# Expert and converted output weights with four consecutive rows per partition

## Chip, cores and metric

The kernel runs on one core of a Trainium2 chip. The metric is device microseconds of one execution, as the median of the runs.

## What is computed

The reference, cut to what matters (the feed-forward weights are float64 in the inputs, the rest float32):

```python
# cross read: B=8, H=8, S=512 tokens, Ns=32 state rows, D=64
a  = softmax(x @ state.T / 8);  xread = a @ state
a2 = softmax(state @ x.T / 8);  sread = a2 @ x
x  = concat([xread, sread])                  # 4352 tokens x 512
# gated unit: d_ff = 1536
xn = x / rms(x) * rms_g
x  = silu(xn @ w_gate) * (xn @ w_val) @ w_out
# soft mixture: 8 experts x 4 slots, hidden 1024
logits = x @ phi                             # 32 slots
d = softmax over tokens;  slot_input = d.T @ x
for e in range(8):
    slot_out[e] = relu(slot_input[e] @ w1[e]) @ w2[e]
out = softmax over slots(logits) @ slot_out
```

## The kernel before

The 4352 tokens are worked through in nine groups: eight of 512 tokens, one for each batch (in steps of 128 tokens by 512 hidden columns), and one of 256 tokens with the state rows that were read. For each step TensorE forms gate and value products, ScalarE and VectorE make the gated hidden rows, TensorE transposes them, and the logits against the slots are accumulated. `w_out` is never applied to the tokens: the slots' sums are taken over hidden rows (`acc`, 128 x 3 x 512), and `w_out` is applied once, to the 32 slots. This is where the change begins.

After the last group comes the tail (L996 and after), which runs in this order:

- `acc` is turned by products with `dsel` (L1024: three chunks of four products, whose stationary side is a block of 128 columns of `acc`), giving `shT`. The converted `w_out` (`take(("wo", c))`, L1030) is applied to it. The result `sip` holds the 32 slots by 512 columns in four partial rows.
- `sip` is turned by four products with `r32` (L1058, stationary side a block of 128 columns of `sip`). L1062 puts each expert's slots into `sinE[e]`, with zeros elsewhere.
- The experts run in four pairs. `expert_in(p)` (L1081) multiplies two experts' slots by `w1`: 16 products of 32 slot columns by 512 hidden columns, on TensorE's four groups of 32 columns. `expert_turn(p)` (L1096) transposes the copies `HP` (eight transposes of 128 columns, stationary side a block of `HP`), `expert_out(p)` (L1112) multiplies by `w2` into `so_ps`. The order is: `expert_in(0)`, then for each p `expert_in(p + 1)`, `expert_turn(p)`, `expert_out(p - 1)`, and at the end `expert_out(3)`.
- The slots' outputs are spread to all tokens (`out0`, `out_group`) and written out.

The weights for the tail come in 35 loads of 1 MB each: three of the converted `w_out` from its place in device memory, 16 of `w1`, 16 of `w2`. They are all issued on SP's queue by `prefetch` (L700) in the order of the list `loads` (L686 to L695). A load is issued when the buffer that it takes has been released: `take` marks the buffer, `refill` issues the next load. Each load puts 512 rows by 512 columns on 128 partitions as four rows of 512 for each partition. Which rows these are is what changes:

```python
# L711, L713, L715: row 128 k + p goes to partition p, place k
src = w_out32[k[1] * 512 : (k[1] + 1) * 512, :].rearrange("(k p) d -> p k d", p=P)
src = w1[k[1], :, k[2] * 512 : (k[2] + 1) * 512].rearrange("(k p) f -> p k f", p=P)
src = w2[k[1], k[2] * 512 : (k[2] + 1) * 512, :].rearrange("(k p) d -> p k d", p=P)
```

Since float32 products are issued as two passes, one `mm` of float32 operands shows as two matmuls and two weight loads in the profile. A transpose shows as one of each.

Of the kernel before, what the change touches and what calls it, by code (L numbers as in the profile page):

```python
# [20 lines left out]
def kernel(  # L21
# [62 lines left out]
    def mm(o, lhsT, rhs, start=True, stop=True):  # L84
        nc.tensor.matmul(out=o, lhsT=lhsT, rhs=rhs, start=start, stop=stop)  # L85

# [1 line left out]
    ident = small("ident", [P, P])  # L88
    make_identity(nc, ident)
    r32 = small("r32", [P, 32])  # L90
# [5 lines left out]
    rs_magic = small("rs_magic", [P, NT], dt=I32)  # L96
    nc.vector.memset(rs_magic.bitcast(F32), RS_MAGIC)

    # Bits of float64's high word, read as float32: the least and greatest that float32 holds.
    EXP_LO, EXP_HI = 2.0 ** -15, 122879.984375  # L100

    def keep_warm(n):
        """Products that nobody reads, so that a short wait doesn't slow the array's clock."""
        ps = mmps()
        for _ in range(n):
            tc.keep_in_program_order(nc.tensor.matmul(out=ps[:, :P], lhsT=ident, rhs=ident, start=True, stop=True))

    def transpose(o, i):
        nc.tensor.transpose(o, i, ident)  # L109

# [1 line left out]
    XN, T = {}, {}  # L112

    def load_xt(b):
# [15 lines left out]
    phis = asmall("phis", [P, 4, NSLOT])  # L130
    nc.scalar.dma_start(out=phis, in_=phi)

# [1 line left out]
    dram = ctx.enter_context(tc.tile_pool(name="dram", bufs=1, space=bass.MemoryType.DRAM))  # L134
    w_out32 = dram.tile([DFF, DM], F32, name="w_out32")
    bits = {
# [84 lines left out]
                )  # L221


# [1 line left out]
    def att_g(b):  # L225
        stTg = small("stTg", [P, P], bufs=3)
        ins = nc.gpsimd.tensor_tensor(
# [173 lines left out]
    RINV = {}  # L401

    def rinv_from(g, ss, n):
        """(ss / DM + 1e-6) ** -0.5, by Newton's steps from the halved exponent."""
        y = small("rinv", [P, NT], bufs=3)[:, :n]
        v = small("rv", [P, NT])[:, :n]
        a = small("ra", [P, NT])[:, :n]
        i = small("ri", [P, NT], dt=I32)[:, :n]
        nc.vector.tensor_scalar(
            out=v, in0=ss, scalar1=1.0 / DM, scalar2=1e-6, op0=ALU.mult, op1=ALU.add  # L410
        )
        nc.vector.tensor_scalar(  # L412
            out=i, in0=v.bitcast(I32), scalar1=1, scalar2=-1,
            op0=ALU.logical_shift_right, op1=ALU.bitwise_xor,
        )
        nc.gpsimd.tensor_tensor(out=y.bitcast(I32), in0=i, in1=rs_magic[:, :n], op=ALU.add)  # L416
        for _ in range(3):
            nc.vector.tensor_tensor(out=a, in0=y, in1=y, op=ALU.mult)
            nc.vector.scalar_tensor_tensor(
                out=a, in0=a, scalar=-0.5, in1=v, op0=ALU.mult, op1=ALU.mult  # L420
            )
            nc.vector.scalar_tensor_tensor(
                out=y, in0=a, scalar=1.5, in1=y, op0=ALU.add, op1=ALU.mult
            )
        RINV[g] = y

# [1 line left out]
    WP = {}  # L428

    def sw(b, c, gv):  # L430
# [14 lines left out]
            )  # L445
        WP[b, c, gv] = t

# [1 line left out]
    HH, HT, LGP = {}, {}, {}  # L449
    xsg_t = {}  # L450
    wphi = small("wphi", [P, NF, 32])
# [56 lines left out]
                stop=(c == NC - 1),  # L508
            )

# [1 line left out]
    sacc = small("sacc", [P, 1])  # L512
    mrun = small("mrun", [P, 1])
    Q = {}
# [103 lines left out]
            out=v, in0=v, in1=cs[:, :n].unsqueeze(2).to_broadcast([P, n, 32]), op=ALU.mult  # L618
        )

# [1 line left out]
    wphi_done, WPP = set(), {}  # L622

    def wphi_part(c, j):
        """phi' @ w_out' for half of the d_model rows of a 512-wide chunk; j = 1 ends the chunk."""
        wt = WOT.pop((c, j))
        ps = misc()
        for k in range(2):
            mm(ps[32 * k : 32 * k + 32, :], phis[:, 2 * j + k, :], wt[:, k, :])
        if j == 0:  # L630
            WPP[c] = k2("wpp")
            nc.vector.tensor_copy(WPP[c][:64], ps[:64])
            return
        wp = WPP.pop(c)
        nc.vector.tensor_tensor(out=wp[:64], in0=ps[:64], in1=wp[:64], op=ALU.add)
        ps = misc()
        for q in range(4):
            mm(ps[:, 32 * q : 32 * q + 32], wp[:64, q * P : (q + 1) * P], r32[:64])
        nc.vector.tensor_copy(
            wphi[:, 4 * c : 4 * c + 4, :], ps[:, :P].rearrange("p (q s) -> p q s", q=4)  # L640
        )
        wphi_done.add(c)

# [1 line left out]
    def sread_prep():  # L645
        xg = k8("xg").rearrange("p a f -> p (a f)")[:, : 4 * B * NS].rearrange(
            "p (k n) -> p k n", k=4
# [23 lines left out]
    WH = {}  # L671

    def w_split(gv, c):
        """The weights' chunk in two float32r parts."""
        w = W.pop((gv, c))
        h, l = k8("wh", F32R), k8("wl", F32R)
        for k in range(4):
            nc.scalar.copy(h[:, k, :], w[:, k, :])
            nc.vector.tensor_tensor(
                out=l[:, k, :], in0=w[:, k, :], in1=h[:, k, :].bitcast(F32), op=ALU.subtract  # L680
            )
        WH[gv, c] = h, l

# [1 line left out]
    EW = {}  # L685
    loads = []  # L686
    for c in range(NC):
# [1 line left out]
    NPAIR = NE // 2  # L689
    for p in range(NPAIR + 2):  # L690
        if p < NPAIR:
            loads += [("w1", 2 * p + i, j) for j in range(2) for i in range(2)]
        if p >= 2:
            loads += [("w2", 2 * (p - 2) + i, j) for i in range(2) for j in range(2)]
    loads.reverse()  # L695
# [2 lines left out]
    ew_home, ew_free = {}, []  # L698

    def prefetch(n, home=None):  # L700
        """Start the next n loads, in slots of `big` (home None) or of the experts' pool."""
        for _ in range(n):
            if not loads:
                return
            k = loads.pop()
            if home is None:
                t = k8("ew")
            else:
                t = home.tile([P, 4, 512], F32, tag="ew", bufs=4, name="ew_" + "_".join(map(str, k)))
            if k[0] == "wo":  # L710
                src = w_out32[k[1] * 512 : (k[1] + 1) * 512, :].rearrange("(k p) d -> p k d", p=P)  # L711
            elif k[0] == "w1":
                src = w1[k[1], :, k[2] * 512 : (k[2] + 1) * 512].rearrange("(k p) f -> p k f", p=P)  # L713
            else:
                src = w2[k[1], k[2] * 512 : (k[2] + 1) * 512, :].rearrange("(k p) d -> p k d", p=P)  # L715
            nc.sync.dma_start(out=t, in_=src)
            EW[k], ew_home[k] = t, home

# [5 lines left out]
        while ew_free:  # L724
            prefetch(1, ew_free.pop(0))

# [1 line left out]
    def conv1(n=1):  # L728
        wconv(n)
        if len(to_load) > 6 and (to_load[-1][0] < 2 or len(RAW) < 3):  # L730
# [39 lines left out]
        rinv_from(0, T[0, "ss"], NT)  # L770

    pinned.append(1)
# [1 line left out]
    def rinv(b):  # L774
        rinv_from(b, T[b, "ss"], NT)

# [22 lines left out]
    for s, units in enumerate(stages):  # L799
# [65 lines left out]
            at(16, 1, att_a4, 2)  # L865
        else:
            g = s
            o = 4 if s == 1 else 0  # the first unit's place in the usual twelve
            if s == 1:
                at(0, 1, conv1)  # L870
                at(0, 2, wphi_part, 2, 1)
# [121 lines left out]
        prefetch(PU[u])  # L993
    assert not plan

# [1 line left out]
    h_T(*pend[0])  # L997
    lg_mm(*pend[0])
    post1(gs)
# [21 lines left out]
    for c in range(NC):  # L1021
        ps = mmps()
        for q in range(4):
            mm(ps[:, 32 * q : 32 * q + 32], acc[:, c, q * P : (q + 1) * P], dsel)  # L1024
        (nc.vector.tensor_copy if c % 2 else nc.scalar.copy)(
            shT[:, 4 * c : 4 * c + 4, :], ps[:, :P].rearrange("p (q s) -> p q s", s=32)
        )
# [27 lines left out]
    c_exp(gs)  # L1055
    ps = misc()
    for k in range(4):
        mm(ps[:, 32 * k : 32 * k + 32], sip[:, k * P : (k + 1) * P], r32)  # L1058
    # each expert's inputs of its own slots, zero in the others'
    for e in range(NE):  # L1060
        es = slice(4 * e, 4 * e + 4)
        nc.vector.tensor_tensor(  # L1062
# [16 lines left out]
    HP = {}  # L1079

    def expert_in(p):  # L1081
        """The first products of two experts: slots of one have zeros in the other."""
        for j in range(2):
            ps = mmps()
            for i in range(2):
                e = 2 * p + i
                wt = take(("w1", e, j))
                for k in range(4):
                    mm(
                        ps[32 * k : 32 * k + 32, :], sinE[e][:, k, :], wt[:, k, :],  # L1090
                        start=(i == 0), stop=(i == 1),
                    )
            HP[p, j] = hp1[:, 2 * (p % 2) + j, :]
            (nc.scalar.copy if j else nc.vector.tensor_copy)(HP[p, j], ps)

    def expert_turn(p):  # L1096
        hr = small("hr", [P, 8, 8], bufs=2)
        for j in range(2):
            ps = misc()
            for q in range(4):  # L1100
                transpose(ps[:, q * P : (q + 1) * P], HP[p, j][:, q * P : (q + 1) * P])
            HP.pop((p, j))
            v = ps.rearrange("p (f k s) -> p f s k", f=4, k=4)[:, :, 8 * p : 8 * p + 8, :]
            nc.vector.reduce_sum(hr[:, 4 * j : 4 * j + 4], v, axis=AX.X)
        for i in range(2):
            e = 2 * p + i
            nc.vector.tensor_scalar(
                out=hzs[e][:, :, 4 * e : 4 * e + 4], in0=hr[:, :, 4 * i : 4 * i + 4],
                scalar1=0.0, scalar2=None, op0=ALU.max,
            )  # L1110
# [10 lines left out]
                    )  # L1121

    def out_prep():
        """Group 0's weights of the slots, in two parts, each four times."""
        ch = k8("ch", F32R)[:, 0, :P].rearrange("p (t s) -> p t s", s=32)
        cs = k8("cs")[:, :2, :].rearrange("p i (t q s) -> p i t q s", t=NT, q=4)
        cr = k8("csT", F32R)
# [83 lines left out]
    c_turn(1)  # L1211
    expert_out(NPAIR - 1)

    # so_ps still has the four parts of each slot's sum; group 0 takes it as it is
    s4 = k8("s4", F32R)
    s4_h, s4_l = s4[:, 0, :], s4[:, 1, :]
    nc.scalar.copy(s4_h, so_ps)
# [86 lines left out]
```

## Time and profile before

| what | us |
|---|---|
| median of 3 runs (lowest, highest) | 690.29 (690.04, 691.79) |
| profiled execution: span from first to last instruction | 691.4 |
| TensorE busy in that span | 640.3 (93%) |
| VectorE busy | 407.7 (59%) |
| ScalarE busy | 388.9 (56%) |
| weight loads of TensorE busy (beside its products) | 410.6 (59%) |
| DMA: 92.55 MB, share of 16 engines on the main queue | 36.3% |

The profiled execution's own time is its span: nothing that is shown lies around it, and the span lies inside the range of the three runs. In the profile, PE is TensorE's products, PEld its weight loads, DVE VectorE, ACT ScalarE, POOL GpSimd and SP the queue that issues the transfers. L1024 is line 1024 of the kernel before. `mm<-dsel,acc` names the output, the moving and the stationary operand, in this order. The chain of waits is followed back from the last instruction to what released it; the time of a stretch on it is time that sets the end.

### The profile page before, as it was taken

Reading aid. Unit: us, or ns where it says so; the run is one execution under the profiler, and the core shown is the slowest. Engines: PE = TensorE matmul, PEld = TensorE weight load, DVE = VectorE, ACT = ScalarE, POOL = GpSimd, SP = SyncE. Lnnn points to the kernel's source line nnn. Section 1 sums busy time; section 2 is a strip of 40 time slices with the busy share of each in tenths; the row PEclk is TensorE's granted clock in tenths of the full one; section 3 lists DMA queues with packets and bytes.
Section 4 is the critical chain, followed back from the end, with each engine's and each line's share of the span. In section 5 each row is a group of like instructions: output and inputs, shape, how many; then the busy total and the mean of one; then the engine's idle time right before and its main releaser. Section 6 shows DMA issues by size and latency. Waiting matters only on the chain.

```text
span 691.4 us, 11529 instructions
## 1 busy us (share of the span) xinstructions
PE 640.3 (93%) x4560; PEld 410.6 (59%) x4560; DVE 407.7 (59%) x852; ACT 388.9 (56%) x632; POOL 129.1 (19%) x158
## 2 busy tenths in 40 slices
PE   6789988999989999999999999999999999999980
PEld 4346646456555766566676658665666676753350
DVE  6979996762687457554835673575455355342160
ACT  5477943754776459546764765496446366311170
POOL 2634554230032101110201021011000000002430
PEclk9799998999999999999999999999999999999995
DMA  9940246031042011203110320020081307999957
GB/s 349 404 193 2 101 152 236 1 129 63 1 156 96 5 47 77 96 5 122 45 53 1 122 92 1 19 105 31 1 309 58 122 1 257 326 334 382 344 186 331
DMA packets 33581, 92.55 MB, mean 134 GB/s; under 512 B 1912, under 2 KB 4088, under 8 KB 30712
## 3 DMA queue, kind: packets, MB, share of 16 engines
q1 hardware_dynamic: 33240, 91.76, 36.3%
q8 instruction: 36, 0.59, 0.4%
q14 instruction: 17, 0.14, 0.1%
q10 hardware_dynamic: 288, 0.07, 0.0%
HBM read 79.76 MB, written 12.06 MB: 133 GB/s over the span
## 4 chain that ended last, share of the span: by engine, by line
PE 75%; DVE 7%; ACT 5%; issue 1%; POOL 0%; DVEq 0%; ACTq 0%
PE mm L85 42%; PE misc L85 17%; PE misc L109 10%; PE lg L85 3%; PE so L85 2%; DVE wp L443 1%; DVE h L479 1%; ACT wp L442 1%; ACT L471 1%; DVE wo L200 1%; ACT sg L471 1%; DVE wo L208 1%; DVE rm L272 1%; ACT sT L285 0%; DVE wo L204 0%
## 5 line engine op out<-in xcount | busy, mean ns | idle before, releaser
L85 PE MATMUL mm<-wp,A 128*128 128x512 f32 x1152 | 304.9, 405 | 0.4 <-DVE h L479 0.4
L85 PEld LDWEIGHTS mm<-wp,A 128*128 128x128 f32 x1152 | 207.3, 189 | 64.1 <-issue 24.5
L479 DVE SCALAR_TENSOR_TENSOR h<-mm,rinv,sg 128x512 f32<-128x512 f32 x102 | 76.1, 747 | 131.1 <-PE mm L85 93.6
L471 ACT ACTIVATE sg<-mm,rinv 128x512 f32<-128x512 f32 x102 | 70.2, 690 | 81.0 <-PE mm L85 78.0
L85 PE MATMUL misc<-w,stTg 64*32 64x512 f32 x768 | 81.7, 618 | 17.6 <-DVE wp L443 7.5
L442 ACT CAST wp<-misc 128x512 fp32r<-128x512 f32 x96 | 51.7, 591 | 65.2 <-PE misc L85 63.1
L443 DVE TENSOR_TENSOR wp<-misc,wp 128x512 fp32r<-128x512 f32 x96 | 61.8, 682 | 26.6 <-ACT wp L442 26.1
L109 PE MATMUL misc<-ident,h 128*128 128x128 f32 x408 | 61.3, 277 | 1.9 <-DVE h L479 0.7
L490 ACT COPY hT<-misc 128x512 f32<-128x512 f32 x86 | 49.2, 580 | 24.6 <-PE misc L109 20.5
L109 PEld LDWEIGHTS misc<-ident,h 128*128 128x128 f32 x408 | 50.1, 142 | 18.2 <-DVE wp L443 3.3
L85 PEld LDWEIGHTS misc<-w,stTg 64*32 64x32 f32 x768 | 15.5, 106 | 67.7 <-issue 22.1
L308 POOL TENSOR_TENSOR a<-a,asum 128x1024 f32<-128x1024 f32 x7 | 13.4, 1917 | 132.4 <-issue 84.8
L471 ACT ACT_TABLE_LOAD x28 | 35.9, 1283 | 3.7 <-PE mm L85 3.2
L416 POOL TENSOR_TENSOR rinv<-ri,rs_magic 128x4 int32<-128x4 int32 (+1 forms) x9 | 1.8, 198 | 173.2 <-DVE ri L412 173.2
L397 ACT ACTIVATE misc<-misc 128x512 f32<-128x512 f32 x32 | 18.7, 585 | 26.9 <-PE misc L85 18.8
L212 POOL TENSOR_TENSOR w<-w,raw 128x512 int32<-128x512 int32 x20 | 28.1, 1418 | 27.6 <-ACT wp L442 7.2
L85 PE MATMUL mm<-wh,xsg 128*128 128x512 f32 x96 | 31.7, 399 | 0.0
L85 PE MATMUL misc<-bd,A 128*128 128x256 f32 x192 | 29.6, 292 | 1.5 <-DVE A L380 1.5
L212 POOL TENSOR_TENSOR wo<-wo,raw 128x512 int32<-128x512 int32 x18 | 24.8, 1387 | 32.7 <-DVE wo L208 23.3
L85 PE MATMUL lg<-hT,wphi 128*32 128x512 f32 (+1 forms) x216 | 27.4, 577 | 1.5 <-ACT hT L490 1.5
L85 PEld LDWEIGHTS misc<-bd,A 128*128 128x128 f32 x192 | 25.5, 191 | 5.1 <-DVE A L380 2.2
L85 PE MATMUL misc<-h,ET 128*32 128x512 f32 x204 | 26.4, 596 | 0.0
(196 smaller groups left out, 831.8 us busy)
## 6 DMA issues: line engine op xcount, KB each, us to landing
ew<-in_w_dram SPq DMA_DIRECT2D x27, 1024.0 KB, 8.1
xT<-in_x_t_dram SPq DMA_DIRECT2D x8, 1024.0 KB, 5.5
xn<-in_x_n_dram SPq DMA_DIRECT2D x8, 1024.0 KB, 7.7
raw<-in_w_val_dram SPq DMA_DIRECT2D x6, 1024.0 KB, 16.6
raw<-in_w_out_dram SPq DMA_DIRECT2D x6, 1024.0 KB, 5.0
out_dram<-ob SPq DMA_DIRECT2D x6, 1024.0 KB, 12.1
ew_w<-in_w_dram SPq DMA_DIRECT2D x5, 1024.0 KB, 10.4
raw<-in_w_gate_dram SPq DMA_DIRECT2D x4, 1024.0 KB, 14.2
```

The lines of the kernel that those rows point to most:

```text
L85: nc.tensor.matmul(out=o, lhsT=lhsT, rhs=rhs, start=start, stop=stop)
L109: nc.tensor.transpose(o, i, ident)
L200: nc.vector.tensor_scalar(out=dst[:, h], in0=dst[:, h], scalar1=EXP_LO, scalar2=EXP_HI, op0=ALU.max, op1=ALU.min,)
L208: nc.vector.scalar_tensor_tensor(out=a[:, h], in0=hi[:, h], scalar=-0x40000000, in1=a[:, h], op0=ALU.bitwise_and, op1=ALU.bitwise_or,)
L212: nc.gpsimd.tensor_tensor(out=a[:, h], in0=a[:, h], in1=rnd[:, h], op=ALU.add)
L308: (eng or nc.gpsimd).tensor_tensor(out=a3, in0=a3, in1=asum.unsqueeze(2).to_broadcast([P, 32, 32]), op=ALU.mult)
L397: nc.scalar.activation(out=ps, in_=ps, func=AF.Square, accum_out=T[b, "ss"][:, t : t + 1])
L442: nc.scalar.copy(t[:, r, 0, :], ps)
L443: nc.vector.tensor_tensor(out=t[:, r, 1, :], in0=ps, in1=t[:, r, 0, :].bitcast(F32), op=ALU.subtract)
L471: nc.scalar.activation(out=sg, in_=ps, func=AF.Silu, scale=RINV[g][:, t : t + 1])
L479: nc.vector.scalar_tensor_tensor(out=HH[g, c][:, t, :], in0=ps, scalar=RINV[g][:, t : t + 1], in1=sg, op0=ALU.mult, op1=ALU.mult,)
L490: (nc.vector.tensor_copy if on_dve else nc.scalar.copy)(HT[g, c][:, :, t * P : (t + 1) * P], ps.rearrange("p (q n) -> p q n", q=4))
```

## The change

The four rows of 512 that one partition holds become consecutive rows of the weight matrix: row 4 p + k instead of row 128 k + p. For `w_out` and `w2` a partition then reads 8 KB in one piece, where it read four pieces of 2 KB. For `w1`, whose rows are 1024 long, a load now holds two whole rows for each partition (j chooses rows 4 p + 2 j and 4 p + 2 j + 1) instead of half of the columns of four rows, and again reads 8 KB in one piece. The product's other side has to follow: the blocks of 128 columns of `acc`, `sip` and `HP` become every fourth column (`every4`). `expert_in` needs both loads of an expert for each half of the hidden columns, so it keeps two accumulators and goes over experts outside and halves inside. The loads of `w1` come in the order of experts. Comments were removed as well.

```diff
+    def every4(rows, k):
+        return rows.rearrange("s (p k) -> s k p", k=4)[:, k, :]
+
...
-            loads += [("w1", 2 * p + i, j) for j in range(2) for i in range(2)]
+            loads += [("w1", 2 * p + i, j) for i in range(2) for j in range(2)]
...
             if k[0] == "wo":
-                src = w_out32[k[1] * 512 : (k[1] + 1) * 512, :].rearrange("(k p) d -> p k d", p=P)
+                src = w_out32[k[1] * 512 : (k[1] + 1) * 512, :].rearrange("(p k) d -> p k d", k=4)
             elif k[0] == "w1":
-                src = w1[k[1], :, k[2] * 512 : (k[2] + 1) * 512].rearrange("(k p) f -> p k f", p=P)
+                src = w1[k[1]].rearrange("(p k) f -> p (k f)", k=4)
+                src = src[:, k[2] * 2048 : (k[2] + 1) * 2048].rearrange("p (k f) -> p k f", k=4)
             else:
-                src = w2[k[1], k[2] * 512 : (k[2] + 1) * 512, :].rearrange("(k p) d -> p k d", p=P)
+                src = w2[k[1], k[2] * 512 : (k[2] + 1) * 512, :].rearrange("(p k) d -> p k d", k=4)
...
-            mm(ps[:, 32 * q : 32 * q + 32], acc[:, c, q * P : (q + 1) * P], dsel)
+            mm(ps[:, 32 * q : 32 * q + 32], every4(acc[:, c, :], q), dsel)
...
-        mm(ps[:, 32 * k : 32 * k + 32], sip[:, k * P : (k + 1) * P], r32)
+        mm(ps[:, 32 * k : 32 * k + 32], every4(sip, k), r32)
...
     def expert_in(p):
-        for j in range(2):
-            ps = mmps()
-            for i in range(2):
-                e = 2 * p + i
-                wt = take(("w1", e, j))
+        pss = [mmps(), mmps()]
+        for i in range(2):
+            e = 2 * p + i
+            wts = [take(("w1", e, j)).rearrange("p (k j) f -> p k j f", j=2) for j in range(2)]
+            for j in range(2):
                 for k in range(4):
                     mm(
-                        ps[32 * k : 32 * k + 32, :], sinE[e][:, k, :], wt[:, k, :],
+                        pss[j][32 * k : 32 * k + 32, :], sinE[e][:, k, :], wts[k // 2][:, k % 2, j, :],
                         start=(i == 0), stop=(i == 1),
                     )
+        for j in range(2):
             HP[p, j] = hp1[:, 2 * (p % 2) + j, :]
-            (nc.scalar.copy if j else nc.vector.tensor_copy)(HP[p, j], ps)
+            (nc.scalar.copy if j else nc.vector.tensor_copy)(HP[p, j], pss[j])
...
-                transpose(ps[:, q * P : (q + 1) * P], HP[p, j][:, q * P : (q + 1) * P])
+                transpose(ps[:, q * P : (q + 1) * P], every4(HP[p, j], q))
```

On TensorE, the products of `expert_in(0)` (names that begin with ew are the buffers of the loads, in the order in which they were issued; in the order of the program):

```order
-L85 MATMUL mm<-ew_w_0_0_4967,sinE 32x512 x4
-L85 MATMUL mm<-ew_5033,sinE 32x512 x4
-L85 MATMUL mm<-ew_5035,sinE 32x512 x4
-L85 MATMUL mm<-ew_5300,sinE 32x512 x4
...
+L85 MATMUL mm<-ew_w_0_0_4967,sinE 32x512 x2
+L85 MATMUL mm<-ew_5033,sinE 32x512 x2
+L85 MATMUL mm<-ew_w_0_0_4967,sinE 32x512 x2
+L85 MATMUL mm<-ew_5033,sinE 32x512 x2
+L85 MATMUL mm<-ew_5035,sinE 32x512 x2
+L85 MATMUL mm<-ew_5300,sinE 32x512 x2
```

Where four products in a row read one load, two now read one load and two the other, and both loads of an expert are in use until its last products. The number of products is as before, and nothing else on TensorE changes its place.

On SP's queue, the loads of the tail (35 rows on each side; one of `w_out`, one of `w1` and one of `w2` stand here, in this order):

```order
-L716 DMA ew_wo_4961<-w_out_89 128x4x512
...
-L716 DMA ew_w_0_0_4967<-in_w_dram 128x4x512
...
-L716 DMA ew_w_2_0_5881<-in_w_dram 128x4x512
...
+L720 DMA ew_wo_4961<-w_out_89 128x2048
...
+L720 DMA ew_w_0_0_4967<-in_w_dram 128x2048
...
+L720 DMA ew_w_2_0_5881<-in_w_dram 128x2048
```

The loads stand in the same places of the queue; each has one run of 2048 elements for each partition where it had four of 512.

## Rows read from the trace of the kernel before

**Rows 1.** Page: span, and 40 slices of it (TensorE, granted clock, DMA).
```profile
span 691.4 us, 11529 instructions
...
PE   6789988999989999999999999999999999999980
...
PEclk9799998999999999999999999999999999999995
```

**Rows 2.** Chain of waits, 603 to 692 us: start us, us, what.
```profile
615.07 1.90 PE mm L85 x16
616.97 0.97 PE misc L85 x2
617.95 1.01 PE mm L85 x8
618.96 2.74 PE misc L85 x22
...
622.20 1.09 PE misc L85 x8
...
623.60 7.07 PE mm L85 x64
630.67 1.02 PE misc L109 x8
631.70 3.57 PE mm L85 x32
...
656.18 1.90 PE so L85 x16
...
673.35 1.12 ACT ob L1179 x2
```

**Rows 3.** Stretches: us, busy PE, PEld, DVE, ACT, POOL; PEclk, DMA share, GB/s.
```profile
605.00:623.00 18.00, 17.42 (x121) 9.75 (x122) 8.44 (x29) 3.05 (x10) 1.05 (x2) 1.00 0.98 335
623.00:658.00 35.00, 34.57 (x305) 12.79 (x304) 7.69 (x29) 3.88 (x7) 13.29 (x40) 1.00 0.95 351
...
625.00:650.00 25.00, 25.00 (x228) 9.17 (x224) 6.26 (x20) 2.34 (x4) 8.17 (x24) 1.00 1.04 384
680.00:685.00 5.00, 0.00 (x0) 0.00 (x0) 0.00 (x0) 0.00 (x0) 0.00 (x0) 0.50 1.00 418
```

**Rows 4.** L85 from 611 to 660 us: what its engine waited for, us, times.
```profile
  DMA ew<-in_w_dram: 0.6, 2
```

**Rows 5.** DMA from 625 to 660 us: busy tenths in 40 slices; issues, us to landing.
```profile
DMA  9999999999999999999999999999999998300000
...
ew<-in_w_dram SPq DMA_DIRECT2D x8, 1024.0 KB, 14.0
```

**Rows 6.** Timeline of the tail: start us, us, engine, line, operation, tiles.
```profile
615.00 1.86 PEld L85 LDWEIGHTS mm<-dsel,acc 128*128 128x128 f32 x16 [0.84 <-DVE acc L598]
622.20 0.97 PEld L85 LDWEIGHTS misc<-r,sip 128*128 128x128 f32 x8 [0.31 <-DVE sip L1045]
630.60 0.86 PEld L109 LDWEIGHTS misc<-ident,hp 128*128 128x128 f32 x8 [0.84 <-DVE hp L1094]
641.64 0.69 DVE L1094 COPY hp<-mm 128x512 f32<-128x512 f32 x1 [4.72 <-PE mm L85]
647.81 0.86 PEld L109 LDWEIGHTS misc<-ident,hp 128*128 128x128 f32 x8 [0.84 <-issue]
```

**Rows 7.** Weight loads by shape: count, busy us, mean ns, idle before.
```profile
L109 PEld LDWEIGHTS misc<-ident,hp 128*128 128x128 f32 x32 | 3.4, 140 | 3.4 <-DVE hp L1094 2.5 <-issue 0.8
L85 PEld LDWEIGHTS mm<-dsel,acc 128*128 128x128 f32 x24 | 2.8, 191 | 1.7 <-DVE shT L1025 0.8 <-DVE acc L598 0.8
...
L85 PEld LDWEIGHTS misc<-r,sip 128*128 128x128 f32 x8 | 1.0, 191 | 0.3 <-DVE sip L1045 0.3
```

**Rows 8.** VectorE by line: duration ns min/median/max, first and last start, shapes.
```profile
L91 DVE TENSOR_REDUCE r<-ident x1: 372/372/372, 1.3 to 1.3; 128x32 f32<-128x128 f32 x1
...
L1010 DVE TENSOR_REDUCE mg<-mm x1: 292/292/292, 611.1 to 611.1; 128x32 f32<-128x128 f32 x1
...
L1025 DVE COPY shT<-mm x1: 290/290/290, 617.0 to 617.0; 128x128 f32<-128x128 f32 x1
...
L1094 DVE COPY hp<-mm x4: 690/691/692, 626.4 to 641.6; 128x512 f32<-128x512 f32 x4
...
L208 DVE SCALAR_TENSOR_TENSOR w<-raw,w x20: 676/680/870, 16.3 to 91.8; 128x512 int32<-128x512 int32 x20
...
L679 DVE TENSOR_TENSOR wl<-w,wh x24: 679/683/693, 561.7 to 594.0; 128x512 fp32r<-128x512 f32 x24
```

**Rows 9.** Chain of waits, a stretch of twelve main products.
```profile
506.58 2.77 PE mm L85 x12
```

## The prediction

> **What bounds the kernel now.** I read the page's slices first [rows 1]. TensorE is busy in nearly all of the span and idle only in the last slices. The change touches the loads of the tail and three places where their products' other side is read, all of them after 604 us, so the chain of waits is read from there [rows 2]. From 615 to 658 us it runs on TensorE almost without a break: products with `acc`, with the converted `w_out`, the turn of `sip`, and then the experts, whose 64 matmuls of the first two pairs take 7.07 us, or 110 ns each, the same as the 112 ns of the next 32. The reader should see that TensorE never slows there for want of data. After 658 us come the outputs; the chain's last piece on an engine ends at 674.5 us, and the rest of the span is the outputs' way out.
>
> The other resource of the tail is the DMA. It is full from 625 to 650 us, share 1.04 at 384 GB/s [rows 3], so a transfer-bound tail looks plausible. Two views say that it is not. Of TensorE's idle time from 611 to 660 us, the share put down to a load is 0.6 us in two pieces [rows 4]. And the queue runs dry before it is needed: the slices of 0.875 us show it full until 653.9 us and empty from 655.6 us [rows 5], while the last two loads are used in the 16 matmuls that start at 656.18 us [rows 2], the very last of them in the second half of these. The slack is 0.6 to 1.5 us, small, but it is slack. **TensorE bounds the tail, and the loads run beside it.**
>
> **The loads.** With 8 KB pieces the outputs leave at 418 GB/s, where the loads in 2 KB pieces come at 384 [rows 3]: an estimate from these two is 2.51 us in place of 2.73 us for a load of 1.049 MB. From 605 to 658 us, 18 us at 335 GB/s and 35 us at 351 hold some 17 loads [rows 3], so the queue could be done about 17 x 0.22 = 3.7 us earlier. All of that is hidden by TensorE. It widens the slack and takes at most the 0.6 us of rows 4 off the path. If a load became dearer instead, cover for it is 14 us from issue to landing [rows 5]; only a loss of more than the slack at the end of the queue would show. I take 0, with -0.6 as one end.
>
> **Order in `expert_in`.** The number of products is unchanged, and four products in a row still go to the four column groups. Buffers are released later: the first load of a pair after 6 of 16 products instead of 4. Sixteen products take 3.57 us as 32 matmuls [rows 2], so this is 0.45 us, hidden in the 14 us that a load waits behind others in the queue. The first half's copy to `HP` starts after 12 products instead of 8, or 0.9 us later. In the last pair that copy started at 641.64 us and took 0.69 us; the transposes that need it start at 647.81 us [rows 6], so 5 us of other products hide it. An expert now needs two loads before its first product instead of one; the queue is more than this ahead, as rows 4 show. All of this costs 0. Were the cover gone, the price is the same 0.9 us per pair.
>
> **The stationary sides.** Every load of weights from `acc`, `sip` and `HP` reads every fourth element: 24 + 8 + 32 = 64 weight loads [rows 7]. They are on the path, and they, not the products, set its pace there. The products with `acc` move 32 columns only, and the loads follow each other every (1.86 - 0.19) / 15 = 111 ns; those of `sip` every (0.97 - 0.19) / 7 = 111 ns, those of `HP` every (0.86 - 0.14) / 7 = 103 ns [rows 6, 7]. Whatever a load takes beyond this comes out at the end.
>
> No weight load of the kernel before has a stride, so the price is bounded by VectorE. At startup L91 reads 128 elements of an on-chip matrix with a stride of 32 and takes 372 ns. L1010, the same reduction with the same stride but from the accumulators, takes 292 ns [rows 8]. So 80 ns more for 128 elements. VectorE takes (690 - 290) / 384 = 1.04 ns for an element in its copies [rows 8], 133 ns for 128; with the 80 ns, an isolated read costs 213 / 128 = 1.66 ns. A second row points to the same size: twelve main products of 512 columns take 2.77 us [rows 9], 231 ns each, so TensorE takes four neighbouring float32 in 1.80 ns, and no row shows it faster. If a fetch of one small piece of neighbours is the unit, an element alone costs as much as four together. With a stride of two there is no penalty: L208 reads every second element of its raw words and takes 680 ns, L679 reads neighbours and takes 683 [rows 8]. Four lies between two and 32; I expect it on the dear side, since the unit of four neighbours would just be left at every step.
>
> [...]
>
> **The sum.** At 1.66 ns a load of 128 columns takes 213 ns: (213 - 111) x 32 = 3.3 us for `acc` and `sip`, (213 - 103) x 32 = 3.5 us for `HP`, together 6.8 us. The ends of this case: 64 x 80 ns = 5.1 us, if only VectorE's difference is added, and (231 - 111) x 32 + (231 - 103) x 32 = 7.9 us by the main products' pace. Free stride: 0. I take 6.8 because it is built from VectorE's isolated read. The profiled span becomes 691.4 + 6.8 = 698.2 us; against the median, 1.1 us below that span, it is 690.3 + 6.8 = **697.1 us**, and 695.4 to 698.2 for this case alone. The outputs just start 6.8 us later: their stage is paced by its own copies and transfers, which the change leaves alone.
>
> **Rivals.** *A stride of four is free* (chance 0.33). Then nothing of the change lies on the path and the time is 690.3, from 689.7 with rows 4's wait gone to 691.0. For it: stride two is free, and a weight load takes 103 to 111 ns for 128 columns, only half of the 2.2 elements per ns at which TensorE reads its moving side (512 / 231), so the load may have room to spare. It decides at a fetch time of about 0.85 ns per element: below it the old pace holds. [...]
>
> *The loads did bind* (0.04). Then faster loads let TensorE run ahead. But the 0.6 us of rows 4 is all that can be had; to get under 688.2, more than 2.1 us would have to be waits that the profile puts down to something else, and TensorE is busy 34.57 of 35 us there [rows 3].
>
> *A little dearer* (0.08): the load's read partly overlaps, a third of the 6.8 us shows, 691 to 695. *Much dearer* (0.05): an isolated read costs twice 213 ns, so 64 x 0.32 = 20 us, 711; no row has such a price.
>
> **Chances and range.** The dear stride (213 ns) 0.50, free 0.33, in between 0.08, much dearer 0.05, faster 0.04. About 0.3% (2.1 us) is what a measurement can tell from no change. Slower: 0.50 + 0.05 and 0.06 of the in-between, 0.61; the same: 0.35; faster 0.04. Since both sides hold much, the range reaches from the free case to the dear end: 689.7 to 698.4 us, which leaves out the much dearer and the faster case.
>
> **What would show it.** Right: the 64 weight loads on `acc`, `sip` and `HP` last longer, eight of `HP` take 1.6 us or more instead of 0.86, and the stretch from the first product on `acc` to the last on `so` grows by 5 to 8 us, while its other rows keep their length. Loads land sooner and the DMA runs dry earlier. Wrong: these loads keep their 0.86 us (free), or waits for a load appear in front of `expert_in`, or the growth stands in the outputs' stage.

## The result, and the profile after

The changed kernel takes **698.86 us** (median of 4 runs, 698.2 to 699.6); the kernel before, on the same chip, 690.16 us. The ratio is 1.0125, with a 95% interval of 1.0108 to 1.0142: 8.7 us slower, and 0.5 us above the predicted range.

The page shows the span and the granted clock in 40 slices:

```profile
span 697.2 us, 11527 instructions
...
PEclk9599989999999999999999999999999999979995
```

In [rows 1] the clock stays up from the eighth slice to the last but one. Here one slice near the end, which begins at about 610 us, has 7.

The chain of waits through the tail (start us, us, what):

```profile
611.74 3.85 PE mm L85 x16
615.59 0.98 PE misc L85 x2
616.56 2.00 PE mm L85 x8
618.57 5.31 PE misc L85 x22
...
623.90 0.44 DVE sip L1049
...
624.36 0.38 ACT sip L1050
...
624.78 2.07 PE misc L85 x8
...
627.16 8.77 PE mm L85 x64
635.93 1.16 PE misc L109 x8
637.09 3.57 PE mm L85 x32
...
662.00 1.90 PE so L85 x16
```

Piece by piece against [rows 2]: the products with `acc` take 3.85 + 2.00 us where they took 1.90 + 1.01 (+2.94). The turn of `sip` takes 2.07 for 1.09 (+0.98) and waits for one more copy, ScalarE's, which was not on the chain before (+0.40). The transposes of `HP` take 1.16 for 1.02, four times (+0.56). So far these are the strided places. But two pieces that read nothing with a stride also grew: the products with `w_out` from 2.74 to 5.31 us (+2.57), and the experts' first 64 matmuls from 7.07 to 8.77 (+1.70). The next 32, at 637.09 us, take 3.57 as before. The sum is 9.15 us, and the stretch from the first product on `acc` to the last on `so` grew from 43.0 to 52.2 us.

Why those two pieces grew is seen in stretches of TensorE (columns as in rows 3; the number before the last two is the granted clock):

```profile
612.00:617.00 5.00, 5.00 (x21) 4.12 (x20) 0.82 (x2) 0.27 (x1) 0.00 (x0) 1.00 0.94 357
617.00:623.70 6.70, 6.70 (x29) 2.41 (x29) 0.00 (x0) 0.27 (x1) 0.00 (x0) 0.50 0.41 144
624.00:627.00 3.00, 2.26 (x10) 2.04 (x9) 0.85 (x4) 0.37 (x1) 0.50 (x1) 1.00 0.98 380
627.20:630.50 3.30, 3.30 (x16) 0.76 (x20) 0.47 (x6) 0.00 (x0) 0.00 (x0) 0.51 0.79 325
631.00:636.00 5.00, 5.00 (x49) 1.44 (x42) 1.38 (x2) 0.58 (x1) 1.66 (x1) 1.00 0.84 311
```

The granted clock falls from 1.00 to about half twice: to 0.50 at 617 us, after the slow products with `acc`, and again at 627 us (0.51 from 627.2 to 630.5 us), after the slow turn of `sip`. Ahead of the first fall TensorE counts as busy without a break (5.00 of 5.00 us, with a weight load running in 4.12 of them). Ahead of the second it is busy in 2.26 of 3.00 us, since there are waits on both sides of the turn.

The weight loads by shape, to set beside [rows 7]:

```profile
L85 PEld LDWEIGHTS mm<-dsel,acc 128*128 128x128 f32 x24 | 5.7, 328 | 1.7 <-DVE shT L1029 0.8 <-DVE acc L598 0.8
L109 PEld LDWEIGHTS misc<-ident,hp 128*128 128x128 f32 x32 | 4.2, 210 | 3.4 <-DVE hp L1099 2.5 <-issue 0.8
L85 PEld LDWEIGHTS misc<-r,sip 128*128 128x128 f32 x8 | 1.9, 327 | 0.7 <-ACT sip L1050 0.7
```

and the time lines of the first group on `acc` and of eight transposes of `HP`. The pace of the loads follows from them as (3.81 - 0.33) / 15 = 232 ns, where it was 111, and (1.04 - 0.21) / 7 = 119 ns, where it was 103:

```profile
611.67 3.81 PEld L85 LDWEIGHTS mm<-dsel,acc 128*128 128x128 f32 x16 [0.84 <-DVE acc L598]
...
635.86 1.04 PEld L109 LDWEIGHTS misc<-ident,hp 128*128 128x128 f32 x8 [0.84 <-DVE hp L1099]
```

### The profile page after: what moved, and what is told of

It reads as the page before. It is cut to its first block, busy times and chain, and to the rows that moved or that the text cites. A ratio compares the mean times of both kernels' runs of the same rounds, so it can differ in the third digit from the quotient of the medians.

```text
span 697.2 us, 11527 instructions
## 1 busy us (share of the span) xinstructions
PE 646.9 (93%) x4560; PEld 416.2 (60%) x4560; DVE 405.4 (58%) x852; ACT 388.6 (56%) x632; POOL 130.8 (19%) x158
## 4 chain that ended last, share of the span: by engine, by line
PE 75%; DVE 7%; ACT 5%; issue 1%; POOL 0%; DVEq 0%; ACTq 0%
PE mm L85 43%; PE misc L85 17%; PE misc L109 9%; PE lg L85 3%; PE so L85 2%; DVE wp L443 2%; DVE h L479 1%; ACT wp L442 1%; ACT L471 1%; DVE wo L208 1%; ACT sg L471 1%; DVE rm L272 1%; ACT sT L285 0%; DVE wo L204 0%; POOL w L212 0%
## 5 line engine op out<-in xcount | busy, mean ns | idle before, releaser
L85 PE MATMUL mm<-wp,A 128*128 128x512 f32 x1152 | 305.7, 406 | 0.4 <-DVE h L479 0.4
L85 PEld LDWEIGHTS mm<-wp,A 128*128 128x128 f32 x1152 | 208.0, 190 | 64.5 <-issue 24.8
L85 PE MATMUL misc<-w,stTg 64*32 64x512 f32 x768 | 80.6, 614 | 17.0 <-DVE wp L443 7.5
L490 ACT COPY hT<-misc 128x512 f32<-128x512 f32 x86 | 49.1, 580 | 22.1 <-PE misc L109 18.0
L85 PEld LDWEIGHTS misc<-w,stTg 64*32 64x32 f32 x768 | 15.5, 106 | 66.1 <-issue 22.3
L85 PE MATMUL misc<-bd,A 128*128 128x256 f32 x192 | 31.1, 303 | 1.5 <-DVE A L380 1.5
L85 PE MATMUL mm<-wh,xsg 128*128 128x512 f32 x96 | 31.7, 399 | 0.0
L85 PEld LDWEIGHTS misc<-bd,A 128*128 128x128 f32 x192 | 27.2, 202 | 5.2 <-DVE A L380 2.2
L85 PE MATMUL lg<-hT,wphi 128*32 128x512 f32 (+1 forms) x216 | 27.4, 577 | 1.5 <-ACT hT L490 1.5
L85 PE MATMUL misc<-h,ET 128*32 128x512 f32 x204 | 26.4, 596 | 0.0
```

Of the source, the lines that this page charges most:

```text
L490: (nc.vector.tensor_copy if on_dve else nc.scalar.copy)(HT[g, c][:, :, t * P : (t + 1) * P], ps.rearrange("p (q n) -> p q n", q=4))
```

## The experiments

Theory A, from the profile after: the strided loads of `acc` and `sip` cost 3.9 us, the later start of the turn of `sip` 0.4, those of `HP` 0.6, and the two falls of the clock that follow cost 4.3 us. The rivals stand in the expectations. Each ratio is to the kernel before, run beside that experiment. The kernels e2, e3, e6, e7, e8 and e9 read other columns than the algorithm needs, as their expectations say.

**e1, the kernel before again.**

> The kernel before, once more, for a profile beside those that follow. Theory A (below): 690.2 us, the stretch from the first product on acc to the last on so 43.0 us, no fall of the clock in it. Any rival: the same.

690.45 us, ratio 1.0006 (0.9992 to 1.0019). Its chain:

```profile
611.64 1.90 PE mm L85 x16
...
620.17 7.07 PE mm L85 x64
...
652.75 1.90 PE so L85 x16
```

From 611.64 to 654.65 us are 43.0 us, as expected. It reaches the tail 3.4 us earlier than the profile shown in [rows 2], and within 0.1 us of the changed kernel. That profile had fallen behind long before the tail: against the changed kernel's profile it is 0.4 us ahead at 107 us (ScalarE's L187 starts at 107.64 us, there at 108.04) and 3.2 us behind at 132 (L490 at 132.09 us, there at 128.91). From 116 to 124 us its granted clock was 0.57, and 1.00 in the changed kernel's. The span of e1 is 688.0 us, so the spans differ by 9.2 us, and all of the loss lies in the tail.

**e2 and e3, the strides taken apart.** e2 has plain blocks of `acc` and `sip`, e3 plain blocks of `HP`. First the edit of e2, then that of e3:

```diff
-            mm(ps[:, 32 * q : 32 * q + 32], every4(acc[:, c, :], q), dsel)
+            mm(ps[:, 32 * q : 32 * q + 32], acc[:, c, q * P : (q + 1) * P], dsel)
...
-        mm(ps[:, 32 * k : 32 * k + 32], every4(sip, k), r32)
+        mm(ps[:, 32 * k : 32 * k + 32], sip[:, k * P : (k + 1) * P], r32)
```

```diff
-                transpose(ps[:, q * P : (q + 1) * P], every4(HP[p, j], q))
+                transpose(ps[:, q * P : (q + 1) * P], HP[p, j][:, q * P : (q + 1) * P])
```

> The changed kernel with plain blocks of 128 columns of acc and sip as stationary sides; HP keeps its stride (the rows of the weights then meet other columns, so the output is another). Theory A: the strided loads of acc and sip cost 3.9 us by themselves, the later start of the turn of sip 0.4, the fall of TensorE's clock that follows 4.3, the strided loads of HP only 0.6. So this run gives 690.2 + 0.6 = 690.8 us, and the clock stays at its upper level from 605 to 655 us. Rival B (the new loads and the order in expert_in slow the experts' first products, 8.77 us where they took 7.07): 690.2 + 1.7 + 0.6 = 692.5 us. Rival C (the prediction's sizes, HP 3.5 us): 693.7 us.

> The changed kernel with plain blocks of HP; acc and sip keep their stride (another output). Theory A: 698.9 - 0.6 = 698.3 us, both falls of the clock still there. Rival C: 698.9 - 3.5 = 695.4 us. Rival B: 698.3 us, as theory A.

e2: 690.69 us, ratio 1.0008 (0.9995 to 1.0020). e3: 698.91 us, ratio 1.0124 (1.0103 to 1.0144). The chain of e2:

```profile
611.65 1.90 PE mm L85 x16
...
615.53 2.74 PE misc L85 x22
...
620.18 7.07 PE mm L85 x64
627.25 1.16 PE misc L109 x8
```

With the new loads and the new `expert_in`, but without the strides of `acc` and `sip`, everything but the transposes is back at its old time: the two pieces that the falls of the clock had stretched take 2.74 and 7.07 us again, and the mean granted clock of the execution is 0.973, for 0.965 in the changed kernel. Rivals B and C fall: `HP` costs 0.14 us for eight transposes, not the 0.9 of the prediction. Taking its stride away in e3 gains nothing that the medians show; in e3's trace the stretch from the first product on `acc` to the last on `so` is 51.6 us for the 52.2 of the changed kernel, so the 0.56 us of the transposes are gone, and both stretched pieces are there (5.31 us with `w_out`, 8.77 for the experts' first).

**e4, wider moving sides.** Is it the slow loads that bring the clock down, or how little is streamed past them?

```diff
+    dsel4 = k2("dsel4")[:, :P]
+    nc.vector.tensor_copy(
+        dsel4.rearrange("p (r s) -> p r s", r=4), dsel.unsqueeze(1).to_broadcast([P, 4, 32])
+    )
...
-            mm(ps[:, 32 * q : 32 * q + 32], every4(acc[:, c, :], q), dsel)
+            mm(ps[:, q * P : (q + 1) * P], every4(acc[:, c, :], q), dsel4)
```

and the same for `sip` with `r32` four times; the copies behind them take the first of the four.

> The changed kernel, its strides kept, with moving sides of 128 columns instead of 32 in the products with acc and sip (dsel and r32 four times side by side). Theory A with the clock falling because these products stream few columns while each waits for its slow weight load: the loads still take 232 ns each, the wider products hide beneath them, the clock stays up, and the time is 698.9 - 4.3 = 694.6 us. Rival D (the clock falls because of the slow weight loads themselves, whatever is streamed): 698.9 us or a little more, the clock at half from 617 us as before.

696.01 us, ratio 1.0086 (1.0063 to 1.0108). The chain:

```profile
612.04 5.80 PE mm L85 x24
617.84 2.76 PE misc L85 x24
...
621.65 2.12 PE misc L85 x8
...
624.07 8.77 PE mm L85 x64
```

The 24 matmuls with `acc` take as long as they did with 32 columns (5.80 us for 3.85 + 2.00), since the loads set their pace: 5.67 us for 24 of 329 ns, or one every (5.67 - 0.33) / 23 = 232 ns. But the first fall is gone: the granted clock is 1.00 from 612 to 624 us. So the slow loads alone do not bring the clock down, and rival D falls for this place. The second fall stayed (0.50 from 625 to 627 us, and 8.77 us for the experts' first), so the time missed the expected 694.6 by 1.4.

The edit did one thing more. In the kernel before and in the changed one, two matmuls with `w_out` run between those with `acc` and take 0.97 us by themselves; here they come behind, and all 24 take 2.76 us where the kernel before needed 0.97 + 2.74. That is 0.95 us which has nothing to do with strides, and it means that the width of the moving side is not the only thing that changed ahead of the first fall.

**e7, plain blocks of `sip` alone.**

```diff
-        mm(ps[:, 32 * k : 32 * k + 32], every4(sip, k), r32)
+        mm(ps[:, 32 * k : 32 * k + 32], sip[:, k * P : (k + 1) * P], r32)
```

> The changed kernel with plain blocks of sip; acc and HP keep their stride (another output). Theory A (each strided group pulls the clock down after itself: acc the first fall, sip the second): the acc products 2.9 us, the first fall's 2.6 us and HP's 0.6 us stay, the turn of sip, its wait and the second fall (1.0 + 0.4 + 1.7) go: 696.4 us. Rival H (the second fall is a consequence of the first and needs no stride in sip): 698.0 us, the experts' first 64 matmuls still 8.8 us.

697.28 us (695.53 to 698.67), ratio 1.0099 (1.0076 to 1.0122).

```profile
612.23 3.87 PE mm L85 x16
616.10 1.85 PE misc L85 x2
617.94 2.01 PE mm L85 x8
619.95 5.31 PE misc L85 x22
...
625.76 1.09 PE misc L85 x8
...
627.16 7.07 PE mm L85 x64
```

The second fall is gone with the stride of `sip` (7.07 us), so rival H falls; e4, which has the second fall without the first, says the same. In this execution the first one began earlier and doubled two more matmuls (1.85 for 0.97 us), which is the 0.9 us over the expectation. The four runs spread over 3.1 us; that falls land elsewhere in the others is likely, but only this one was traced.

The traces also show what the half clock leaves alone. In e7 the eight slow matmuls on `acc` that start at 617.94 us stand between two pieces that take about twice their time in the kernel before (1.85 us for 0.97, 5.31 for 2.74), and yet take 2.01 us for the 2.00 of the changed kernel. There the granted clock is 0.53 to 0.50 from 617 us on, and the loads of these eight, from 616.49 us, take 1.94 us in all, one every (1.94 - 0.33) / 7 = 230 ns. The eight loads of `sip`, at a granted clock of 1.00, take the same 1.94 us, and the first sixteen on `acc` were at 232 ns: the strided loads are paced alike at either.

**e10, wider moving sides and the waits filled.** e4 had kept the waits around the turn of `sip`, in which TensorE is mostly idle (busy in 0.35 us of the one from 621 to 622 us). Here `keep_warm(n)`, which the kernel has already, fills them with n products of the identity with itself, 128 columns wide.

The edit, on top of that of e4:

```diff
+    keep_warm(4)
     sinE = []
...
+    keep_warm(2)
     for e in range(NE):
         es = slice(4 * e, 4 * e + 4)
```

> The kernel with moving sides of 128 columns (696.0 us, one fall of the clock left, after the turn of sip), with products that nobody reads in the two short waits around the turn of sip (four before it, two behind it). Theory A, in the form that the clock follows how many columns the array streams, waits included: the second fall goes too, the experts' first 64 matmuls take 7.07 us again, and the time is 696.0 - 1.7 = 694.3 us, less some tenths if these products delay nothing. What is left over 690.2 is then the price of the strides alone at the upper clock, 3.9 + 0.4 = 4.3 us, with HP 0.6. Rival K (the second fall has another cause, such as the strided loads of sip): 696.0 us or more, 8.77 us for these matmuls.

694.48 us, ratio 1.0067 (1.0043 to 1.0091), as expected. The chain:

```profile
612.46 5.80 PE mm L85 x24
618.26 2.71 PE misc L85 x24
...
622.28 1.89 PE misc L85 x8
...
624.62 7.00 PE mm L85 x64
...
657.66 1.90 PE so L85 x16
```

All strides are still there, and their loads as slow as before (5.68 us for the 24 on `acc`, 1.94 for the eight on `sip`; in e4 5.67 and 1.94), but the granted clock is 1.00 from 605 to 640 us: rival K falls. Wide moving sides alone (e4) had not done this behind `sip`, where the clock was 0.50.

The difference of 698.9 - 694.5 = 4.4 us is not the price of the falls alone, though it comes close to their 4.27 us by luck. The stretch from the first product on `acc` to the last on `so` is 47.1 us, 5.1 less than in the changed kernel. The falls are 4.27 of that, and the 24 matmuls with `w_out`, again in one piece, another 1.0; the two waits, now filled, are longer by 0.55, and the rest is in small pieces. The price of the strides and of their wait is better read from the changed kernel's own chain: 2.94 + 0.98 + 0.56 + 0.40 = 4.88 us.

**e6 and e9, strides of two and of three.** In e6 `every4` is this, for all three places:

```diff
-        return rows.rearrange("s (p k) -> s k p", k=4)[:, k, :]
+        return rows.rearrange("s (p k) -> s k p", k=2)[:, k % 2, (k // 2) * P : (k // 2 + 1) * P]
```

In e9 this takes the place of `every4` for `acc` and `sip`, and `HP` is as in e3:

```diff
+    def every3(rows, k):
+        return rows[:, :384].rearrange("s (p k) -> s k p", k=3)[:, k % 3, :]
```

> The changed kernel with a stride of two instead of four in all three places (two interleaved blocks, then the next two; another output). Theory A (the fetch brings several neighbours, four of them in the 231 ns per 512 of the main products; with a stride of two a fetch still gives two): the loads of acc and sip keep to about 111 to 120 ns, the clock stays up, 690.3 to 691.3 us. Rival G (any stride costs): loads of 232 ns, both falls of the clock, 698.9 us.

> The changed kernel with a stride of three in acc and sip (three interleaved blocks of the first 384 columns, the fourth product takes the first block again) and plain blocks of HP (another output). Theory A (a fetch brings four neighbours and takes 1.80 ns, whatever of them is used): 128 elements lie in 96 fetches, 173 ns a load against 111 plain, 118 at stride two and 232 at stride four; 32 loads make 2.0 us, the later start of the turn of sip 0.4, together 692.5 us if the clock stays up. Rival J (the price steps up at four and three is still free): 690.2 to 690.8 us. Rival G' (above two the full price): 698.3 us as with plain HP before.

e6: 691.15 us, ratio 1.0014 (1.0003 to 1.0025). e9: 695.67 us (694.22 to 697.59), ratio 1.0079 (1.0054 to 1.0104). The same sixteen loads on their time lines, first of e6, then of e9:

```profile
613.04 1.96 PEld L85 LDWEIGHTS mm<-dsel,acc 128*128 128x128 f32 x16 [0.84 <-DVE acc L598]
```

```profile
611.99 2.87 PEld L85 LDWEIGHTS mm<-dsel,acc 128*128 128x128 f32 x16 [0.84 <-DVE acc L598]
```

With mean durations of 196 and 262 ns the paces are (1.96 - 0.20) / 15 = 118 ns and (2.87 - 0.26) / 15 = 174 ns. Theory A's 111 to 120 and 173 hold. With 111 plain and 232 at four, the four paces come out within 3 ns as the longer of the plain 111 ns and 128 x stride / 4 times 1.80 ns (115, 173 and 230 at two, three and four). The 1.80 ns is the author's estimate from the 231 ns of [rows 9]; that a load fetches in this way is not shown. Rivals G, G' and J fall. The time of e9 was above the expected 692.5, because at a stride of three the clock fell too (0.69 granted from 616 to 619 us and 0.74 from 619 to 622; its products with `w_out` take 4.25 us for 2.74). That explains the traced run, 694.2 us, the fastest of the four; the rest of the median was not traced. The transposes of `HP` cost the same 1.16 us for eight in e6 as with a stride of four, so their price does not fit that sum, and why is open.

**e5, the new loads without strides.** The copies that fill `acc`, `sip` and `HP` put every fourth column together:

```diff
-                out=acc[:np_, c, :], in0=acc[:np_, c, :], scalar=Q[g, "al"][:np_],
-                in1=ps[:np_, :], op0=ALU.mult, op1=ALU.add,
+                out=acc[:np_, c, :].rearrange("p (k m) -> p k m", k=4),
+                in0=acc[:np_, c, :].rearrange("p (k m) -> p k m", k=4),
+                scalar=Q[g, "al"][:np_],
+                in1=ps[:np_, :].rearrange("p (m k) -> p k m", k=4), op0=ALU.mult, op1=ALU.add,
```

and so for the first copy to `acc` and the copies to `sip` and `HP`; the stationary sides are plain blocks.

> The changed loads, but no stride on TensorE's stationary sides: the copies out of the accumulators that fill acc, sip and HP put every fourth column together, so that plain blocks of 128 hold what every4 took. The output is the reference's. Theory A (the loads in 8 KB pieces were hidden and are worth nothing): 690.3 us, as before, with the last load landing some 4 us before it is used. Rival E (the loads had a gain that the strides hid): under 688.2 us. Rival F (VectorE's and ScalarE's reads of the accumulators with a stride of four are dear): over 692.4 us, with the acc and HP copies longer than 0.74 and 0.69 us.

689.90 us, ratio 0.9996 (0.9985 to 1.0007). The DMA's slices of 0.875 us from 620 to 655 us, of e5 and then of e1:

```profile
DMA  9999999999999999999999999999999931000000
```

```profile
DMA  9999999999999999999999999999999999962000
```

The new loads are done three slices or 2.6 us sooner, and nothing comes of it: rival E falls. VectorE's sums into `acc` take 739 ns in both and its copies to `HP` 691 or 692, so a stride of four in reads of the accumulators is free here, and rival F falls. This is the changed kernel mended, no slower than the kernel before and not measurably faster.

**e8, the strides without the new loads.** The kernel before with `every4` in the three places.

```diff
-            mm(ps[:, 32 * q : 32 * q + 32], acc[:, c, q * P : (q + 1) * P], dsel)
+            mm(ps[:, 32 * q : 32 * q + 32], every4(acc[:, c, :], q), dsel)
...
-        mm(ps[:, 32 * k : 32 * k + 32], sip[:, k * P : (k + 1) * P], r32)
+        mm(ps[:, 32 * k : 32 * k + 32], every4(sip, k), r32)
...
-                transpose(ps[:, q * P : (q + 1) * P], HP[p, j][:, q * P : (q + 1) * P])
+                transpose(ps[:, q * P : (q + 1) * P], every4(HP[p, j], q))
```

> The kernel before, with its loads, list and expert_in as they were, but with every fourth column of acc, sip and HP as stationary sides (another output). Theory A (the strides make the whole of it): 690.3 + 9.1 = 699.4 us at most and 698.9 like the changed kernel. Rival B (the new loads or the new order in expert_in have a part): 697.2 us or less.

699.97 us, ratio 1.0140 (1.0126 to 1.0154), which overlaps the changed kernel's interval. The chain:

```profile
612.38 3.85 PE mm L85 x16
...
619.22 5.31 PE misc L85 x22
...
627.81 8.77 PE mm L85 x64
...
662.64 1.90 PE so L85 x16
```

From 612.38 to 664.54 us are 52.16 us, the same as in the changed kernel (611.74 to 663.90). The strides make the whole of the loss, and rival B falls. The median lies 0.6 us above theory A's upper number; in the trace this kernel reaches the tail 0.64 us later than the changed kernel, so that difference lies ahead of the loads' use.

## Why the prediction was right and wrong

The direction and the place were right: TensorE bounds the tail, the loads are hidden (e5, e2), and a stride of four makes the weight loads of `acc` and `sip` slow, as in the likeliest case, "the dear stride". The mechanism was incomplete. The sum of 6.8 us stood for slow loads alone; the chain grew by 9.15, and nearly half of that is TensorE's clock, which the prediction left out.

- **The loads: 0, right.** The queue ends earlier (2.6 us in e5 for the predicted 3.7), hidden as predicted.
- **Order in `expert_in`: 0, right.** e2 has that order and the old times.
- **`acc` and `sip`: mis-sized.** 213 ns from VectorE's isolated read, measured 232. The step said "I take 6.8 because it is built from VectorE's isolated read"; the other row, TensorE's own four neighbours in 1.80 ns, was the right measure (231), and it was TensorE's. The term was 3.3 us and came to 3.92.
- **`HP`: wrong by a factor of six.** 3.5 us predicted, 0.56 measured. The sum treated a transpose's weight load like any other. Its pace went from 103 to 119 ns only, and eight took 1.04 us, not the 1.6 or more that was to be the sign; why is open.
- **A wait that was not seen.** Each plain block of `sip` came from one of two copies, so the turn began while ScalarE still made the second (both start at 622.2 us in the kernel before, and the copy takes 0.37 us). Every fourth column needs both: +0.40 us. The prediction looked for such waits in `expert_in` and not here.
- **The clock: no term at all.** The stretch was to grow "while its other rows keep their length". They did not. The two falls, from 1.00 to 0.50 and 0.51, cost 4.27 us on the chain (2.57 for the products with `w_out`, 1.70 for the experts' first), and e10, where neither comes, has both pieces back. This is the step that failed. What the prediction could have seen: the `acc` products stream only 32 columns against each load, so a load twice as long leaves an engine that counts as busy (5.00 of 5.00 us from 612 us) and does half as much (the same 24 matmuls in 5.85 us for 2.91); and [rows 1] show that the clock does fall in this kernel, in the early slices (7 in the second, 8 in the seventh).

The over-sized `HP` term (2.9 us too much) hid most of the missing clock term (4.3 us). That the forecast came as near as 1.8 us is luck.

The rival *a stride of four is free* falls with the loads of `acc` and `sip`: 232 ns at four, against 111 plain, 118 at two and 174 at three.

The profiled span of the kernel before was also taken as that execution's whole time, 1.1 us above the median. The later spans lie 1.8 us below their own run's time (697.2 for 698.95), and the first profile, which reaches the tail 3.4 us later than e1, had lost most of this by 132 us, around its stretch at a granted clock of 0.57. Where a change touches only the tail, the stretch of the tail is the better measure.

## What to carry to other kernels

Price a strided stationary side by the engine's own stream: find how long TensorE takes for a few neighbouring elements, and ask whether that exceeds the plain load's pace. Here four came out at an estimated 1.80 ns, or 231 ns for a load of 128 single ones against 111 plain, and 232 was measured; the transposes' loads, 119 ns, did not follow. Then ask what the slower products leave the engine doing, and look at the granted clock behind them: here it fell from 1.00 to 0.50 after a stretch of products 32 columns wide behind slow loads, and the dense work behind it took 5.31 us for 2.74. Where a layout has to be turned, turn it in a copy out of the accumulators that is made anyway: in e5 that was free (739 ns for the sums into `acc` and 691 or 692 for the copies to `HP`, with and without the stride).

## What the hardware showed that was not expected

- Loads of 128 float32 columns were paced at 111, 118, 174 and 232 ns at strides of one, two (e6), three (e9) and four, and the last at 230 ns with the granted clock at about 0.50 (the changed kernel, from 617 us).
- A stride of four costs a transpose's weight load 16 ns (103 to 119), and eight transposes take 1.16 us at a stride of two (e6) as at four, for 1.02 plain.
- TensorE's granted clock fell from 1.00 to 0.50 at 617 us while the engine counted as busy without a break (5.00 of 5.00 us). Four times wider moving sides cost nothing behind the slow loads (5.80 us for 5.85 in e4), and with them, and two matmuls with `w_out` moved, the clock stayed at 1.00 after `acc` (612 to 624 us). After `sip` it took products in the idle waits as well (e10, 1.00 from 605 to 640 us).
